# Outputs issued from ScalarE's DMA queue, and batch 1's norms from GpSimd sums, in a fused cross-covariance attention and three-way maxout FFN

## The chip, the cores and the metric

One core of one Trainium2 chip. The metric is the device time of one execution in microseconds (us). The kernel before takes 574.16 us (median of runs, 574.00 to 574.34).

## The reference, cut to what matters

```python
# q, k, v: (4, 6144, 256) float32; w1, w2, w3: (256, 768); w_out: (768, 256)
qn = q / (norm(q, axis=1) + 1e-6);  kn = k / (norm(k, axis=1) + 1e-6)
a  = softmax(kn.T @ qn / tau)                    # 256 x 256 a batch
x  = (v @ a).reshape(24576, 256)
out = max(x @ w1, x @ w2, x @ w3) @ w_out        # float32
```

The kernel folds `a` into the three weights (the "ew" products give `aw`), so a token needs only `v @ aw` and the output product. The tokens of a batch come in 12 chunks of 512. The Gram matrix `k.T @ q` of the next batch (one burst of products) and its norms are worked out while the chunks of this batch run.

## The kernel before

The steps that matter, cut (`...` marks cuts). Each engine executes its own instructions in the order in which this code issues them.

```python
def norms(b):                                # used for batch 1 only
    n_ps = htile("n_ps")
    accq, acck = accs.pop((b, 0)), accs.pop((b, 1))
    PE.matmul(n_ps[:, :C], lhsT=ones_f, rhs=acck[:, 0:C], ...)
    for j in range(CC):
        PE.matmul(n_ps[:, C + j:C + j + 1], lhsT=accq[:, j * P:(j + 1) * P], rhs=ones_f[:, 0:1], ...)
    ln = sm.tile([P, C + CC], FP32, name="ln")
    ...
def sum_all(b):                              # norms of batches 2 and 3
    ...
    POOL.partition_all_reduce(tot, acc[:, 0:C], P, bass_isa.ReduceOp.add)

def h_block(gi, aw, fc, ...):                # six of these a chunk
    for m in range(3):
        ... PE.matmul(h_ps, lhsT=aw[m][:, ic, fsl], rhs=vt[:, tsl, ic, :], ...)      # 2 x 512 columns
    ACT.activation(out=s_mx, in_=hp[0], func=AF.Copy)                 # "h copy"
    DVE.tensor_tensor(out=s_mx, in0=hp[1], in1=s_mx, op=ALU.max)      # first maximum
    DVE.tensor_tensor(out=ht, in0=hp[2], in1=s_mx, op=ALU.max)        # second maximum

def step(t):                                 # output product, t = 0..3, one in each gap between h blocks
    ...
    if t % 2 == 1:
        ACT.activation(out=st["o"][:, t - 1:t + 1, :], in_=st["ps"], func=AF.Copy)   # "o copy"
    if t == TPC - 1:
        parts = 2 if gi >= B * NCH - 7 else 1
        for i in range(parts):
            SP.dma_start(out=out_r[...], in_=st["o"][:, i * w:(i + 1) * w, :])

def v_transpose(gi):                         # SBUF to SBUF, through the DMA
    SP.dma_start_transpose(out=vt_tile(gi), in_=v_sb.rearrange("p t c -> p (t c)"))
...
if gi == 1:
    hold_loads(2)     # GpSimd copies one element of vt(2): it issues no load before transpose 2 has landed
    load_v(4); load_v(5)
...
l0 = ch if early else ch - 1                 # early = b > 0
if more and 0 <= l0 < 8:
    load_k(b + 1, l0 * 6, 6); load_q(b + 1, l0 * 6, 6)       # cast to fp8, issued by GpSimd
s0 = ch - 2 if early else ch - 3             # the first squares of batch 1 stand in chunk 3
...  square_piece(b + 1, which, g)           # ScalarE squares 3 token groups, GpSimd adds them up
```

Six PSUM buffers hold the h products (two blocks). SBUF pools are laid out one after the other in the order in which they are opened: the small tiles (`sm`, with `ln`), then `v`, `vt`, `ht`, `mx`, `o`.

## Time and profile before

| | before |
|---|---|
| time, us | 574.16 |
| profiled span, us (granted clock) | 572.1 (1.000) |
| TensorE's waits that come after the first batch's loads | none over 0.3 us |
| outputs of ScalarE's / SyncE's queue, MB (of 25.2 written) | 0.1 / the rest |

The page's third part lists DMA queues as packets, MB, and the share of 16 engines' time that the packets took. Before, transposes and outputs share SyncE's queue, and ScalarE has one output, the last:

```profile
q1 hardware_dynamic: 57696, 38.41, 23.7%
q10 hardware_dynamic: 144, 0.13, 0.1%
```

The lines of TensorE's busy share, its chain and its waits are in the prediction below.

### The profile page before, as it was taken

How to read it: one execution, taken by the hardware profiler on the slowest of the kernel's cores; microseconds unless marked ns; L12 is line 12 of the kernel's file. 1: busy time of each engine (PE TensorE's matmuls, PEld its weight loads, DVE VectorE, ACT ScalarE, POOL GpSimd, SP SyncE). 2: the span in 40 equal slices, each digit the busy share in tenths (PEclk: the TensorE clock that was granted, in tenths of full speed). 3: DMA queues.
4: the chain of work that ended last, by engine and by line, in shares of the span. 5: the costliest groups of instructions: out<-in, count | busy, mean ns of one | idle time of the engine just before them, and what ended most of it. 6: DMA issues, size and time to landing. Idle time of an engine off the chain costs nothing.

```text
span 572.1 us, 9442 instructions
## 1 busy us (share of the span) xinstructions
PE 553.9 (97%) x3349; PEld 330.7 (58%) x3350; DVE 411.1 (72%) x647; ACT 309.1 (54%) x539; POOL 235.1 (41%) x240
## 2 busy tenths in 40 slices
PE   3799999999999999999999999999999999999997
PEld 2665555555755555555575555555575555555566
DVE  0048777877577777777768777777868778778775
ACT  1044567677454576776545467767645444444443
POOL 2443357776730078776560048777750000000000
PEclk9999999999999999999999999999999999999999
DMA  9998998884598168984179339885437323132112
GB/s 143 106 146 129 136 237 126 159 135 116 99 107 160 56 107 158 134 148 110 57 128 151 99 81 140 148 141 98 124 86 154 75 75 109 56 103 64 56 55 76
DMA packets 76960, 65.64 MB, mean 115 GB/s; under 512 B 52464, under 2 KB 62576, under 8 KB 76784
## 3 DMA queue, kind: packets, MB, share of 16 engines
q0 software_dynamic: 19072, 26.48, 38.7%
q1 hardware_dynamic: 57696, 38.41, 23.7%
q8 instruction: 26, 0.43, 0.3%
q14 instruction: 22, 0.18, 0.1%
q10 hardware_dynamic: 144, 0.13, 0.1%
HBM read 78.64 MB, written 25.17 MB: 181 GB/s over the span
## 4 chain that ended last, share of the span: by engine, by line
PE 93%; DMA 5%; POOL 0%; issue 0%; DVE 0%; POOLq 0%
PE h_ps L389 65%; PE o_ps L409 22%; DMA q_sb<-in_q_dram 5%; PE gram L260 3%; PE ew_ps L311 3%; POOL k_sb L99 0%; PE o_ps L434 0%; PE ew_ps L335 0%; PE warm_ps L469 0%; PE vt_ps L372 0%; PE gram L177 0%; PE n_ps L215 0%; DVE ht_sb L395 0%; DVE o_sb L461 0%; PE n_ps L217 0%
## 5 line engine op out<-in xcount | busy, mean ns | idle before, releaser
L389 PE MATMUL h_ps<-vt_sb,aw_sb 128*128 128x512 bf16 (+1 forms) x1764 | 406.7, 375 | 0.1
L389 PEld LDWEIGHTS <-aw_sb 128*128 128x128 bf16 x1764 | 171.8, 98 | 161.3 <-DVE aw_sb L317 2.0
L394 DVE TENSOR_TENSOR s_mx<-h_ps,s_mx 128x512 bf16<-128x512 f32 (+1 forms) x294 | 198.7, 676 | 87.1 <-ACT s_mx L393 86.8
L393 ACT ACTIVATE s_mx<-h_ps 128x512 bf16<-128x512 f32 (+1 forms) x294 | 172.4, 587 | 124.9 <-PE h_ps L389 124.0
L395 DVE TENSOR_TENSOR ht_sb<-h_ps,s_mx 128x512 bf16<-128x512 f32 (+1 forms) x294 | 200.2, 681 | 31.4 <-PE o_ps L409 0.5
L203 POOL TENSOR_TENSOR acc<-acc,sq 128x768 f32<-128x768 f32 x90 | 147.6, 1651 | 70.5 <-ACT sq L197 61.6
L409 PE MATMUL o_ps<-wo_sb,ht_sb 128*128 128x256 bf16 x1128 | 153.9, 273 | 0.0
L409 PEld LDWEIGHTS <-ht_sb 128*128 128x128 bf16 x1128 | 110.4, 98 | 52.0
L412 ACT ACTIVATE o_sb<-o_ps 128x512 f32<-128x512 f32 x94 | 56.1, 597 | 85.3 <-PE o_ps L409 85.3
L110 POOL DMA_DIRECT2D v_sb<-in_v_dram x48 | 27.5, 578 | 37.7 <-DMA vt_sb<-v_sb 35.5
L197 ACT ACTIVATE sq<-q_sb 128x768 bf16<-128x768 fp8e4 x48 | 40.5, 845 | 0.0
L197 ACT ACTIVATE sq<-k_sb 128x768 bf16<-128x768 fp8e4 x48 | 40.1, 835 | 0.0
L200 POOL CAST acc<-sq 128x768 f32<-128x768 bf16 x6 | 4.9, 823 | 68.7 <-ACT sq L197 68.7
L102 POOL DMA_DIRECT2D q_sb<-in_q_dram x33 | 18.4, 564 | 5.1 <-DMA v_sb<-in_v_dram 4.1
L165 PE MATMUL kk<-k_sb 128*128 128x256 fp8e4 x48 | 7.5, 338 | 11.9 <-DVE k_sb L151 6.3
L99 POOL DMA_DIRECT2D k_sb<-in_k_dram x29 | 16.1, 555 | 3.1 <-DMA v_sb<-in_v_dram 1.2
L260 PE MATMUL gram<-k_sb,q_sb 128*128 128x512 fp8e4 x144 | 16.8, 277 | 0.0
L260 PEld LDWEIGHTS <-q_sb 128*128 128x256 fp8e4 x144 | 15.9, 136 | 0.6
L314 ACT ACTIVATE aw_sb<-ew_ps,rinv 128x384 bf16<-128x384 f32 (+1 forms) x24 | 13.2, 555 | 5.5 <-PE ew_ps L311 4.7
L311 PE MATMUL ew_ps<-w_sb,et 128*128 128x384 bf16 (+1 forms) x96 | 15.6, 313 | 0.0
L177 PE MATMUL gram<-k_sb,q_sb 128*128 128x512 fp8e4 x48 | 11.4, 332 | 2.6 <-DMA q_sb<-in_q_dram 2.4
L165 PEld LDWEIGHTS <-k_sb 128*128 128x256 fp8e4 x48 | 6.4, 182 | 12.9 <-DMA k_sb<-in_k_dram 6.6
(67 smaller groups left out, 112.9 us busy)
## 6 DMA issues: line engine op xcount, KB each, us to landing
out_dram<-o_sb SPq DMA_DIRECT2D x41, 512.0 KB, 2.9
v_sb<-in_v_dram POOLq DMA_DIRECT2D x48, 256.0 KB, 4.2
k_sb<-in_k_dram POOLq DMA_DIRECT2D x24, 192.0 KB, 6.0
q_sb<-in_q_dram POOLq DMA_DIRECT2D x24, 192.0 KB, 7.6
out_dram<-o_sb SPq DMA_DIRECT2D x13, 256.0 KB, 2.0
k_sb<-in_k_dram POOLq DMA_DIRECT2D x5, 256.0 KB, 10.8
w_sb<-in_moe_w_dram POOLq DMA_DIRECT2D x9, 128.0 KB, 5.7
kf<-in_k_dram SPq DMA_DIRECT2D x1, 1024.0 KB, 4.8
```

The costliest lines, as they stand in the source:

```text
L102: POOL.dma_start(out=qk[b][0][:, g0:g0 + w, :], in_=q_r[b][:, g0:g0 + w, :])
L110: POOL.dma_start(out=t, in_=v_r[gi // NCH, gi % NCH])
L197: ACT.activation(out=sq, in_=src, func=AF.Square)
L203: POOL.tensor_tensor(out=acc, in0=acc, in1=sq, op=ALU.add)
L260: PE.matmul(g[:, j * C:(j + 1) * C], lhsT=qt[:, tsl, j * P:(j + 1) * P], rhs=kt[:, tsl, :], start=(tp == 0 and j == 0), stop=(tp == NG // ...
L311: PE.matmul(ew[:, :w], lhsT=et[:, j, ic * P:(ic + 1) * P], rhs=w_sb[m][:, j, fsl], start=(j == 0), stop=(j == CC - 1))
L389: PE.matmul(t.rearrange("p (t n) -> p t n", n=P), lhsT=aw[m][:, ic, fsl], rhs=vt[:, tsl, ic, :], start=(ic == 0), stop=(ic == CC - 1))
L393: ACT.activation(out=s_mx, in_=hp[0], func=AF.Copy)
L394: DVE.tensor_tensor(out=s_mx, in0=hp[1], in1=s_mx, op=ALU.max)
L395: DVE.tensor_tensor(out=ht, in0=hp[2], in1=s_mx, op=ALU.max)
L409: PE.matmul(st["ps"][:, half], lhsT=ht[:, fc, t * P:(t + 1) * P], rhs=wo_sb[:, fc, :], start=(fc == 0), stop=(fc == FC - 1))
L412: ACT.activation(out=st["o"][:, t - 1:t + 1, :].rearrange("p t d -> p (t d)"), in_=st["ps"], func=AF.Copy)
```

## The change

The intent: SyncE's queue is free of outputs, so that an output no longer stands behind a blocked transpose issue; and the fp32 norm products of batch 1 leave TensorE, which bounds the kernel. For the second, batch 1's squares begin a chunk earlier (chunk 2), so that GpSimd's sums are ready by the Gram burst.

```diff
-    def norms(b):
-        n_ps = htile("n_ps")
-        ...                                  # the n_ps products, the tile ln, three activations
-    def norms_all(b):
+    def norms(b):                            # now for all batches, from sum_all
...
-                    SP.dma_start(out=out_r[gi // NCH, gi % NCH, :, i * w:(i + 1) * w, :],
+                    ACT.dma_start(out=out_r[gi // NCH, gi % NCH, :, i * w:(i + 1) * w, :],
...
+            pieces = [(which, g) for g in range(0, NG, SQW) for which in (1, 0)]
...
-            s0 = ch - 2 if early else ch - 3
-            ...
+            if more and 2 <= ch < 10:
+                at = {2: (3, 4, 5), 3: (0, 1, 2, 3, 5)}.get(ch, (0, 2, 3, 5)) if b == 0 else (0, 2, 3, 5)
+                for f in at:
+                    which, g = pieces.pop(0)
+                    gaps[f].append(lambda which=which, g=g: square_piece(b + 1, which, g))
+                if ch == 9:
+                    gaps[5].append(lambda: (fold(b + 1), sum_all(b + 1)))
```

More of the change, by code (lines that the diff above doesn't have):

```diff
@@ L209, in fold @@
                 POOL.tensor_tensor(out=acc[:, 0:C], in0=acc[:, 0:C], in1=acc[:, i * C:(i + 1) * C], op=ALU.add)
-    def norms(b):
-        n_ps = htile("n_ps")
-        accq, acck = accs.pop((b, 0)), accs.pop((b, 1))
-        PE.matmul(n_ps[:, :C], lhsT=ones_f, rhs=acck[:, 0:C], start=True, stop=False, skip_group_check=True)
-        for j in range(CC):
-            PE.matmul(n_ps[:, C + j:C + j + 1], lhsT=accq[:, j * P:(j + 1) * P], rhs=ones_f[:, 0:1],
-                      start=False, stop=(j == CC - 1), skip_group_check=True)
-        ln = sm.tile([P, C + CC], FP32, name="ln")
-        rkb = sm.tile([P, C], FP32, name="rkb")
-        rq = sm.tile([P, CC], FP32, name="rq")
-        ACT.activation(out=ln, in_=n_ps[:, :C + CC], func=AF.Ln)
-        ACT.activation(out=rkb, in_=ln[:, :C], func=AF.Exp, scale=-0.5)
-        ACT.activation(out=rq, in_=ln[:, C:], func=AF.Exp, scale=-0.5, bias=neg_ln_tau)
-        return rkb, rq
     def sum_all(b):
@@ L504 @@
             v_transpose(gi + 3)
-            early = b > 0
-            l0 = ch if early else ch - 1
+            l0 = ch if b > 0 else ch - 1
             if more and 0 <= l0 < 8:
@@ L518 @@
                 gaps[s + 1].append(f)
-            s0 = ch - 2 if early else ch - 3
-            if more and 0 <= s0 < 8:
-                g0 = s0 * 6
-                for i, (which, g) in enumerate(((1, g0), (1, g0 + SQW), (0, g0), (0, g0 + SQW))):
-                    gaps[(0, 2, 3, 5)[i]].append(lambda which=which, g=g: square_piece(b + 1, which, g))
-            if more and s0 == 7:
-                gaps[5].append(lambda: fold(b + 1))
-                if early:
-                    gaps[5].append(lambda: sum_all(b + 1))
-            if more and ch == NCH - 1:
-                if early:
-                    st["in"] = scaled(gs, st["n"][0])
-                    gaps[0].append(lambda: st.update(e=exp_t(st["in"], st["n"][1])))
-                else:
-                    gaps[0].append(lambda: st.update(n=norms(b + 1)))
-                    gaps[1].append(lambda: st.update({"in": scaled(gs, st["n"][0])}))
-                    gaps[2].append(lambda: st.update(e=exp_t(st["in"], st["n"][1])))
+            if more and 2 <= ch < 10:
[5 more added lines that the diff above has]
+                    gaps[5].append(lambda: (fold(b + 1), sum_all(b + 1)))
+            if more and ch == NCH - 1:
+                st["in"] = scaled(gs, st["n"][0])
+                gaps[0].append(lambda: st.update(e=exp_t(st["in"], st["n"][1])))
                 gaps[4].append(lambda: st.update(r=rowsums(st["e"])))
@@ L543 @@
                 st = {}
-                if early:
-                    st["n"] = norms_all(b + 1)
+                st["n"] = norms(b + 1)
                 gs = gram_kq(b + 1)
```

## The prediction

> **What bounds the kernel now.** I read the page first, then TensorE's waits, then the order of time in four places: a quiet chunk, a batch boundary, the start and the end.
>
> ```profile
> PE 553.9 (97%) x3349; PEld 330.7 (58%) x3350; DVE 411.1 (72%) x647; ACT 309.1 (54%) x539; POOL 235.1 (41%) x240
> PE 93%; DMA 5%; POOL 0%; issue 0%; DVE 0%; POOLq 0%
> PE kk L165 <- DVE k_sb L151: 6.3, 1, 6.3
> PE kk L165 <- DMA k_sb<-in_k_dram: 5.7, 5, 1.6
> PE gram L177 <- DMA q_sb<-in_q_dram: 2.4, 3, 1.2
> ```
>
> TensorE is busy 97% of 572.1 us, the chain that ended last lies on it for 93%, and its whole list of waits is these three lines, all at the first batch's loads. The strip of the granted clock reads 9 in every slice, so throttling is out. A matmul of 512 columns starts every 0.216 us (six take 1.29 us in the chain). From about 37 to 560 us the kernel lasts as long as TensorE's own instructions. Only two things can change the time: fewer TensorE instructions, or new holes between them. ScalarE at 54% looks free, but the share does not say how late one of its copies may be.
>
> **What the Trainium skill says.** "Perfetto Trace Analysis", section "DMA Instruction — HWDGE (DVE, Sync)": the profiler reports a DMA issue until the sequencer is free for its next instruction, and before that the sequencer takes the descriptor generator for itself alone. The first half fits: SyncE's issues take 0.33 us here and its next instruction comes about 0.1 us later. The lock is not shown: at the end an issue of SyncE starts inside one of ScalarE and still takes 0.33 us. "DMA: Bandwidth & Descriptors", section "Issuing engines are not separate DMA queues": issuing from another engine saves only the issue time. So nothing moves faster for coming from ScalarE. The same page, section "Queues, rings and completion order": each DMA engine takes turns between queues, packet by packet. The start agrees: one transpose issue takes 13.83 us while GpSimd's casting loads fill the engines.
>
> **Part 1, batch 1's norms: a gain of 0.8 us.** The n_ps products go (three in the code; the trace records each of these fp32 products twice):
>
> ```profile
> 157.19 1.47 PE L389 MATMUL h_ps<-vt_sb,aw_sb 128*128 128x512 bf16 x6
> 158.49 0.59 PE L215 MATMUL n_ps<-acc,ones_f 128*128 128x256 f32 x2
> 158.92 0.50 PE L217 MATMUL n_ps<-ones_f,acc 128*128 128x1 f32 x4
> 159.29 1.45 PE L389 MATMUL h_ps<-vt_sb,aw_sb 128*128 128x512 bf16 x6
> ```
>
> From 158.49 to 159.29 is 0.80 us. It can be checked: from the start of the Gram burst to the first regular block of three takes 152.10 to 181.70 = 29.60 us for batch 1, but 286.90 to 315.70 = 28.80 us for batch 2, which already uses the GpSimd sums. In batch 2 ScalarE waits 4.9 us for the sums, inside a burst of 5.24 us, and TensorE does not notice. The new work on GpSimd (two all-reduces of 1.81 and 1.88 us) is hidden likewise.
>
> **Part 2, outputs on ScalarE: a loss.** 46 chunks now store from ScalarE's in-order stream, between the second copy of the output and the next h copy:
>
> ```profile
> 480.72 4.05 PE L389 MATMUL h_ps<-vt_sb,aw_sb 128*128 128x512 bf16 x18
> 480.92 0.60 ACT L412 ACTIVATE o_sb<-o_ps 128x512 f32<-128x512 f32 x1 [0.92 <-PE o_ps L409]
> 481.41 0.59 ACT L393 ACTIVATE s_mx<-h_ps 128x512 bf16<-128x512 f32 x1
> 481.54 0.33 SPq L418 DMA_DIRECT2D out_dram<-o_sb  x1
> 482.03 0.69 DVE L394 TENSOR_TENSOR s_mx<-h_ps,s_mx 128x512 bf16<-128x512 f32 x1 [0.52 <-ACT s_mx L393]
> 482.83 0.69 DVE L395 TENSOR_TENSOR ht_sb<-h_ps,s_mx 128x512 bf16<-128x512 f32 x1
> ...
> 568.89 0.41 ACTq L462 DMA_DIRECT2D out_dram<-o_sb  x1
> ```
>
> The store needs the copy's end (481.52), so it starts at 481.54. ScalarE's one issue took 0.41 us, so it ends at 481.95; with 0.1 us to the next start (SyncE's gap, an estimate) the h copy starts at 482.05 in place of 481.41: 0.64 us late. Is there room? The six h buffers hold two blocks. The 18 matmuls are three blocks, and the third takes the first one's buffers. Its last pair starts at 480.72 + 16 x 0.216 = 484.17 and needs the end of the second maximum. That moves: copy 482.05 to 482.64, first maximum 482.66 to 483.35, second 483.46 to 484.15, and a hand-over of 0.02 to 0.05 us after it. The room is just used up: a hole of 0.03 us a chunk. An issue 0.1 us longer or shorter makes it 0.13 or none. With squares in the stream the offsets are the same (140.95, 142.37 against a block starting at 140.26).
>
> Counting the 46: three are followed by a Gram burst, which hides the delay; three fall at a boundary; three at the start; 37 are regular. 37 x 0.03 = 1.1 us (0 to 5).
>
> Boundaries: the sixth ew product starts at about 170.10 and waits for the second maximum of the block before it:
>
> ```profile
> 167.28 0.60 ACT L412 ACTIVATE o_sb<-o_ps 128x512 f32<-128x512 f32 x1 [0.92 <-PE o_ps L409]
> 167.81 0.60 ACT L393 ACTIVATE s_mx<-h_ps 128x512 bf16<-128x512 f32 x1
> 168.44 0.69 DVE L394 TENSOR_TENSOR s_mx<-h_ps,s_mx 128x512 bf16<-128x512 f32 x1 [0.20 <-ACT s_mx L393]
> 169.24 0.69 DVE L395 TENSOR_TENSOR ht_sb<-h_ps,s_mx 128x512 bf16<-128x512 f32 x1
> ```
>
> Now it ends at 169.93. The h copy moves from 167.81 to 168.42, the maximum's end to 170.52: 0.45 us late, three times: 1.3 us. At the end of the kernel VectorE is the bound of the last half chunk, and the same 0.6 us goes straight into the time.
>
> Start: in chunk 2 a square of 0.84 us now also stands behind the store, so the h copy is 0.64 + 0.74 (a square less its overlap) = 1.4 us late, a hole of 0.8 us; chunks 1 and 3 add some 0.3 us, as issues take 0.58 us there.
>
> Sum: -0.8 + 1.1 + 1.3 + 0.6 + 1.1 = +3.3 us, or 577.6 us.
>
> **Rivals.** First, all fits and only the gain remains: 573.5 us. For it: every delay but the boundaries' is within 0.1 us of its room, and only one issue on ScalarE has been measured. Against it: the boundaries and the end have no room at all.
>
> Second, the descriptor generator is taken for the whole of a blocked transpose issue, as the skill words it:
>
> ```profile
> 58.27 0.60 POOL L99 DMA_DIRECT2D k_sb<-in_k_dram  x1
> 61.39 0.61 SPq L418 DMA_DIRECT2D out_dram<-o_sb  x1
> 62.13 13.83 SPq L365 DMA_TRANSPOSE vt_sb<-v_sb  x1
> 76.01 0.58 SPq L418 DMA_DIRECT2D out_dram<-o_sb  x1
> ```
>
> Chunk 1's store falls due near 68.35, inside that issue. ScalarE would stand until the transpose gets through, by my estimate near 73 us (batch 1's third pair of loads now comes behind GpSimd's first sums, so the load queue runs dry earlier than in the kernel before). The hole would be about 5 us in place of 0.8: 582 us. For it: 13.83 us shows that such a block exists. Against it: ScalarE has its own queue, and the overlap of issues at the end.
>
> Third, the squares, one chunk earlier, wait for their loads. Batch 1's first k load was issued at 56.71 and landed 8.2 us later, near 64.9; the first square now comes due at 64.91, with 0.46 us of room before the next h copy. Later a load has a whole chunk of 10.4 us against 6.0 to 7.6 us to landing. I expect under 0.5 us from it, 576 to 580 us in all if it goes wrong.
>
> **Range and chances.** I give the first rival 3 in 10, my sum 4 in 10, the blocked start 3 in 10: a middle of 577.0 us and a range of 573.2 to 583.0 us. Only 0.8 us of TensorE's work goes, so faster by over 2% (562.8) has no source: 0.01. Slower by over 2% (585.8) needs regular holes of 0.25 us or a blocked start longer than estimated: 0.06. Within 2%: 0.93.
>
> **What would show it.** Right: n_ps is gone and the first boundary is 0.8 us shorter but for a hole of some 0.45 us before the sixth ew product; about 47 output issues of 0.4 us on ScalarE; new lines in TensorE's waits naming VectorE's second maximum, a few hundredths of a us in regular chunks, the largest one near 70 us. The second rival: one ScalarE issue of several us near 68. The third: ScalarE's squares waiting for k or q loads. Wrong: issues on ScalarE well away from 0.41 us, TensorE's waits unchanged, or a changed granted clock.

## The result, and the profile after

The changed kernel takes 578.36 us (578.13 to 578.61, four runs) against 574.16: ratio 1.0073 (95% interval 1.0056 to 1.0091), so the same within 2%, and 0.7% slower. A ratio here is the mean time of one kernel's fast runs over that of the other's in the same rounds, so not quite the ratio of the medians quoted. Executions over 1.5% slower than the fastest of the same kernel are left out of the means. The profiled span grew from 572.1 to 576.8 us, 4.7 us.

The page of the changed kernel (busy us, share, instructions; the chain that ended last; the queues):

```profile
PE 555.2 (96%) x3344; PEld 328.9 (57%) x3344; DVE 409.3 (71%) x651; ACT 311.5 (54%) x540; POOL 238.4 (41%) x242
PE 85%; DMA 8%; issue 3%; DVE 1%; POOL 1%; ACT 0%; POOLq 0%; DVEq 0%
q1 hardware_dynamic: 50064, 13.77, 14.4%
q10 hardware_dynamic: 7776, 24.78, 11.7%
```

24.65 MB of outputs (24.78 - 0.13) have moved from SyncE's queue to ScalarE's. TensorE has the same work to do. Its share of the chain fell by 8 points, 46 us, far more than the 4.7 us lost: from the late load at 69 us (below) the chain now runs back through DMA, the transposes and GpSimd, and no longer through TensorE. TensorE's list of waits, beside those for the first loads, now has three lines that the kernel before lacks (us in total, times, longest):

```profile
PE h_ps L373 <- ACT s_mx L377: 1.4, 4, 0.8
PE h_ps L373 <- DVE aw_sb L301: 0.7, 3, 0.2
PE h_ps L373 <- DVE ht_sb L379: 0.2, 1, 0.2
```

They are the places where the time went, but not all of it: a list of waits counts from the modelled end of the product before. I therefore went through TensorE's products in order and added up by how much each start-to-start distance exceeds the usual one of its kind (0.216 us for 512 columns), in both traces. The difference of the two sums, place by place:

| place | us |
|---|---|
| n_ps products gone | -0.80 |
| first loads (before 40 us; the first h product starts at 37.5 to 38.1 us in the six traces, so it differs from run to run) | +0.54 |
| the wait for wo_sb, the weights of the output product, at 51.4 us | +0.19 |
| the start, 70 to 74 us | +2.30 |
| the three batch boundaries (0.57, 0.58, 0.58 against 0.055 each) | +1.56 |
| the end (1.46 against 0.55) | +0.91 |
| regular chunks: no hole over 0.02 us | 0 |
| sum | +4.70 |

The sum is the whole difference of the spans; without the first loads it is 4.16, and the medians differ by 4.20. The three places, one by one.

**The start.** ScalarE's and TensorE's order of time around 70 us (start, us, engine, line, what, and in brackets how long it stood idle and for what); the last line is the kernel before at the same place:

```profile
69.11 0.84 ACT L197 ACTIVATE sq<-k_sb 128x768 bf16<-128x768 fp8e4 x1 [3.47 <-DMA k_sb<-in_k_dram]
70.96 0.34 ACTq L402 DMA_DIRECT2D out_dram<-o_sb  x1
71.41 0.84 ACT L197 ACTIVATE sq<-q_sb 128x768 bf16<-128x768 fp8e4 x1 [0.49 <-DMA q_sb<-in_q_dram]
```

```profile
68.26 1.46 PE L373 MATMUL h_ps<-vt_sb,aw_sb 128*128 128x512 bf16 x6
70.49 1.32 PE L373 MATMUL h_ps<-vt_sb,aw_sb 128*128 128x512 bf16 x4 [0.77 <-ACT s_mx L377]
```

```profile
67.53 4.05 PE L389 MATMUL h_ps<-vt_sb,aw_sb 128*128 128x512 bf16 x18
```

ScalarE stood 3.47 us before batch 1's first square, because its k load had not landed; h copy, o copy and the output stood behind it, and TensorE, whose 18 products ran in one piece before, was held by the missing h copy. This load was issued at 59.06 us and landed at 69.09; before, it was issued at 56.71 and landed at 64.89. It is both issued 2.35 us later and 1.85 us longer under way. The experiments take up why.

During all this SyncE was inside one transpose issue:

```profile
63.93 11.03 SPq L349 DMA_TRANSPOSE vt_sb<-v_sb  x1
```

ScalarE's issue at 70.96 lies in the middle of it and took 0.34 us. So here the issue of one engine did not wait for the blocked issue of another.

**The boundaries.** ScalarE, VectorE and TensorE at the first boundary after the change; the last fence is TensorE before:

```profile
170.15 0.34 ACTq L402 DMA_DIRECT2D out_dram<-o_sb  x1
170.59 0.60 ACT L377 ACTIVATE s_mx<-h_ps 128x512 bf16<-128x512 f32 x1 [0.47 <-PE h_ps L373]
172.62 1.66 DVE L301 TENSOR_SCALAR aw_sb<-ew_ps,rinv 128x384 bf16<-128x384 f32 x3
173.29 1.44 PE L373 MATMUL h_ps<-vt_sb,aw_sb 128*128 128x512 bf16 x5 [0.24 <-DVE aw_sb L301]
```

```profile
170.43 1.52 PE L389 MATMUL h_ps<-vt_sb,aw_sb 128*128 128x512 bf16 x6
```

No ew product waits: the sixth pair starts at 172.34 us, before the second maximum of the block before it has ended (172.70). The issue makes the h copy late, the h copy makes VectorE's two maxima late, and VectorE's scaling of the new weights comes after them in its order. The next batch's first products need those weights: the run of six is broken after its first product.

**The end.** The last two runs of products, TensorE and ScalarE after, TensorE before:

```profile
560.09 0.38 PE L373 MATMUL h_ps<-vt_sb,aw_sb 128*128 128x256 bf16 x2 [0.23 <-ACT s_mx L377]
565.10 0.96 ACTq L402 DMA_DIRECT2D out_dram<-o_sb  x2
566.16 0.66 ACT L377 ACTIVATE s_mx<-h_ps 128x256 bf16<-128x256 f32 x2 [0.47 <-PE h_ps L373]
566.59 3.42 PE L373 MATMUL h_ps<-vt_sb,aw_sb 128*128 128x256 bf16 x24 [0.23 <-ACT s_mx L377]
```

```profile
553.45 2.77 PE L389 MATMUL h_ps<-vt_sb,aw_sb 128*128 128x512 bf16 x18
560.64 4.63 PE L389 MATMUL h_ps<-vt_sb,aw_sb 128*128 128x256 bf16 x36
```

There are two places. At 560.09, where the products turn from 512 to 256 columns and a run of 18 was in one piece before, there is now a hole of 0.42 us. In the last half chunk the 36 products in one piece have become 12 and 24 with a hole between, and smaller holes follow inside the 24 (1.04 us in all, against 0.55 before). Two output issues stand ahead of the h copy of 566.16, but they cost no more than one: the first (565.10 to 565.44) falls within the o copy of 565.09 to 565.69, and the h copy starts 1.07 us after the o copy, as in a regular chunk (1.06, below).

**A regular chunk.** Near 485 us:

```profile
484.76 0.60 ACT L396 ACTIVATE o_sb<-o_ps 128x512 f32<-128x512 f32 x1 [0.92 <-PE o_ps L393]
485.38 0.34 ACTq L402 DMA_DIRECT2D out_dram<-o_sb  x1
485.82 1.26 ACT L377 ACTIVATE s_mx<-h_ps 128x512 bf16<-128x512 f32 x2 [0.47 <-PE h_ps L373]
```

The h copy starts 1.06 us after the o copy in place of 0.49: 0.57 us late. TensorE does not notice.

### The profile page after: what moved, and what is told of

It is laid out like the page before. It is cut to its first block, busy times and chain, and to the rows that moved or that the text cites. A ratio compares the mean times of both kernels' runs of the same rounds, so it can differ in the third digit from the quotient of the medians.

```text
span 576.8 us, 9433 instructions
## 1 busy us (share of the span) xinstructions
PE 555.2 (96%) x3344; PEld 328.9 (57%) x3344; DVE 409.3 (71%) x651; ACT 311.5 (54%) x540; POOL 238.4 (41%) x242
## 3 DMA queue, kind: packets, MB, share of 16 engines
q10 hardware_dynamic: 7776, 24.78, 11.7%
## 4 chain that ended last, share of the span: by engine, by line
PE 85%; DMA 8%; issue 3%; DVE 1%; POOL 1%; ACT 0%; POOLq 0%; DVEq 0%
PE h_ps L373 61%; PE o_ps L393 20%; DMA v_sb<-in_v_dram 4%; PE gram L244 3%; DMA k_sb<-in_k_dram 2%; DMA vt_sb<-v_sb 1%; PE ew_ps L295 1%; DMA q_sb<-in_q_dram 1%; DVE s_mx L378 1%; DVE ht_sb L379 0%; POOL k_sb L99 0%; PE o_ps L418 0%; ACT s_mx L377 0%; DVE aw_sb L301 0%; POOL v_sb L110 0%
## 5 line engine op out<-in xcount | busy, mean ns | idle before, releaser
L110 POOL DMA_DIRECT2D v_sb<-in_v_dram x48 | 27.7, 583 | 28.1 <-DMA vt_sb<-v_sb 25.9
L216 POOL PARTITION_ALL_REDUCE tot<-acc x6 | 10.8, 1844 | 18.2 <-issue 12.1
```

The costliest lines, as they stand in the source:

```text
L110: POOL.dma_start(out=t, in_=v_r[gi // NCH, gi % NCH])
```

## The experiments

The first four ran on one chip, beside 11 runs of the kernel before (median 574.06 us, 573.84 to 574.49).

**store_sp: the change without the move of the outputs.**

```diff
-                    ACT.dma_start(out=out_r[...],
+                    SP.dma_start(out=out_r[...],
```

> The changed kernel with its output stores back on SyncE; the norms from GpSimd and the early squares stay. My theory (a store in ScalarE's stream makes the next h copy about 0.57 us late, and chunk 1's output in a queue of its own holds up batch 1's first k load): the holes of 0.52 us at the three boundaries and of 0.9 us at the end are gone, the k load lands some 8 us after its issue instead of 10, and the hole of 2.3 us near 70 us shrinks to under 0.3 us: 573.4 us, 0.8 us below the kernel before. Rival 1, the boundary holes come from the removed n_ps product, which changed the order of the PSUM buffers: they stay, 575 us. Rival 2, the squares come too early whatever the queue: most of the 2.3 us stays, 575.5 us.

Measured: 573.43, 573.53, 573.59 and 573.65 us in four runs, 581.48 in the profiled one and 597.35 in one that counts as slow; ratio of the fast runs 1.0018 (0.9977 to 1.0059), so the same within 2% as the kernel before. In its trace the boundaries have no hole over 0.1 us, the end has 0.55 us again, and there is no hole near 70 us: the boundary and end losses belong to the outputs' place in ScalarE's stream. The load landed 7.65 us after its issue, and the first square waited 1.00 us for it, though the squares stood as early as in the changed kernel. The four good runs have no trace. Their mean, 573.55 us, is 4.8 us below the changed kernel's time, and the start, the boundaries and the end together lost 4.77, so by their times all three losses are gone. They lie 0.5 us below the kernel before; 0.8 was expected from n_ps. The profiled run lost its time elsewhere, in a way that no run of the kernel before or of the changed one shows in its time:

```profile
98.42 0.84 ACT L197 ACTIVATE sq<-k_sb 128x768 bf16<-128x768 fp8e4 x1 [6.05 <-DMA k_sb<-in_k_dram]
99.80 1.01 PE L373 MATMUL h_ps<-vt_sb,aw_sb 128*128 128x512 bf16 x2 [4.39 <-ACT s_mx L377]
101.89 2.67 PE L373 MATMUL h_ps<-vt_sb,aw_sb 128*128 128x512 bf16 x6
```

A square waited 6.05 us for its load, TensorE stood 4.39 us behind it, and after that six products took 2.67 us in place of 1.46: the granted clock was 0.5 for some 6.8 us. That agrees with the Trainium skill, "TensorE: Matmul & The Clock Gate", section "What's actually happening", by which the clock falls to half after an idle window of about 3.4 us; shorter holes (1.48 us at 84.9 us in the same trace) left it at 1. The DMA queues of 85 to 100 us go one step further back, first this run, then the kernel before (packets, MB, share of 16 engines):

```profile
q1 hardware_dynamic: 2302, 1.55, 85.5%
```

```profile
q1 hardware_dynamic: 1200, 0.79, 19.7%
```

The packets of transposes and outputs took 0.855 x 15 us x 16 / 2302 = 89 ns each, against 39 ns. Sorted by size in the trace, it is the transposes' 256-byte packets that are longer: 82.9 ns in the mean against 24.0 (and 27.7 in the changed kernel); the outputs' packets of 4096 bytes took 166 ns against 174. The loads beside them landed 14 to 18 us after their issue in place of 4 to 8. I call this the congested state below.

**store_only: only the move, in the kernel before.**

```diff
-                    SP.dma_start(out=out_r[...],
+                    ACT.dma_start(out=out_r[...],
```

> The kernel before with nothing but its output stores moved to ScalarE. My theory: boundary holes of about 0.5 us three times and about 0.9 us at the end, no hole near 70 us because no square waits for an early load there: 574.2 + 1.5 + 0.9 = 576.6 us. If the stores alone made the start hole as well (an issue that blocks, or chunk 2's late copy), 578.9 us. If the boundary holes come from the removed product, 575.1 us.

Measured: 578.44, 580.96, 581.08, 581.44 us, and 588.51 in the profiled run (slow); ratio 1.0111 (1.0095 to 1.0127). The trace has the holes of the boundaries (0.51, 0.57, 0.57) and of the end (1.72, against 1.46 in the changed kernel), so they need nothing of the norms. But the time misses the expected 576.6: the best run is 1.8 us above it. The profiled run was congested as well. One square waited 8.44 us for a k load, and TensorE behind it:

```profile
155.26 1.01 PE L389 MATMUL h_ps<-vt_sb,aw_sb 128*128 128x512 bf16 x2 [7.34 <-ACT s_mx L393]
```

The trace also shows what can have lifted the best run. At 81.3 us there is a hole of 2.05 us, in which TensorE waited for a transposed v tile, as it never does in the kernel before:

```profile
PE h_ps L389 <- DMA vt_sb<-v_sb: 1.9, 1, 1.9
```

That transpose landed at 81.25 us (78.33 before). An estimate from these traces, 574.06 + 1.48 (boundaries) + 0.91 to 1.17 (end) + 2.05, gives 578.5 to 578.8 us, and the best run took 578.44; it has no trace, so this is a fit and no more.

**late_squares: the changed kernel with batch 1's first squares back in chunk 3.**

```diff
-                at = {2: (3, 4, 5), 3: (0, 1, 2, 3, 5)}.get(ch, (0, 2, 3, 5)) if b == 0 else (0, 2, 3, 5)
+                at = {2: (), 3: (0, 1, 2, 3, 5), 4: (0, 1, 2, 3, 5), 5: (0, 1, 2, 3, 5), 6: (0, 1, 2, 3, 5)}.get(ch, (0, 2, 3, 5)) if b == 0 else (0, 2, 3, 5)
```

> The changed kernel, but batch 1's squares start in chunk 3 as in the kernel before (five in each of chunks 3 to 6, four in 7 to 9), stores stay on ScalarE. My theory: the hole of 2.3 us near 70 us goes and the rest stays: 578.3 - 2.3 = 576.0 us. Rival, the store of chunk 1 or 2 blocks ScalarE by itself: the hole stays, 578 us. A second way to miss: five squares a chunk crowd ScalarE or GpSimd and the sums arrive after the Gram burst, over 578 us.

Measured: 577.74, 578.11, 581.03, 585.94 us, and two slow runs of 586.51 and 591.07, the latter profiled; ratio 1.0115 (1.0072 to 1.0158). A miss as a time. In the trace the hole near 70 us is gone, as expected; in its place stand others. Those from 109 us on, one of 7.15 us at 127 us, come behind squares that wait for their loads (8.5 us at the most), that is, the congested state. The first, 2.33 us at 82.2 us, is that of store_only again, a transpose that landed at 82.17:

```profile
PE h_ps L373 <- DMA vt_sb<-v_sb: 2.2, 1, 2.2
```

So in this trace the loss of the start was not gone but had moved, from a square's load to a transpose, at the same size. The best two runs, 577.74 and 578.11, gain only 0.3 to 0.6 us on the changed kernel, which fits that; they have no trace.

**late_squares_sp: the same with the outputs back on SyncE.**

```diff
-                    ACT.dma_start(out=out_r[...],
+                    SP.dma_start(out=out_r[...],                # and the edit of late_squares
```

> Both undone: stores on SyncE and the squares from chunk 3, only the norms from GpSimd stay. All theories: the 0.80 us of the removed product alone, 573.4 us or a ratio of 0.9986 to the kernel before; first boundary 28.8 us from the start of the Gram burst to the first regular block of three. If it isn't below the kernel before, the gain of the removed product was given back elsewhere in the burst.

Measured: 584.90, 585.19, 586.77, 589.05 us and a slow 597.31; ratio 1.0215 (1.0194 to 1.0237), a verdict of unclear at the bound of 2%. The clearest miss: no run came near the 573.5 us of store_sp, whose outputs it has. It differs from store_sp only in where the squares stand, and by its times it lost over 10 us in all five runs, where store_sp did so in one of six and 8 us in another. So the squares' places bear on the congested state; how is not shown. In the trace ScalarE waits 15.1 us in four places for k loads, and TensorE has holes between 80 and 127 us, but none at the boundaries.

**What these four leave.** They settle the boundaries and the end. For the start, the three traces with outputs from ScalarE lose 2.30, 2.05 and 2.33 us before 85 us, by a late square or a late transpose; with outputs from SyncE none is lost near 70 us in any, and at the transposes' place near 80 us none in two traces and 0.65 in late_squares_sp (store_sp's congestion begins at 84.9). They don't say why the changed kernel's first load comes late. Two things can be read side by side from the six traces.

First, the transposes. SyncE's first transpose runs alone, and the second holds up GpSimd, which issues batch 1's first load only after its guard copy. In the kernel before, the first takes (us from issue to landing), and the guard copies stand at (first and last start):

```profile
vt_sb<-v_sb SPq DMA_TRANSPOSE x1, 2.9
L480 POOL COPY guard<-vt_sb x2: 185/186/188, 45.1 to 54.7; 128x1 bf16<-128x1 bf16 x2
```

In the changed kernel, the first, the second, and the guard copies:

```profile
vt_sb<-v_sb SPq DMA_TRANSPOSE x1, 3.2
vt_sb<-v_sb SPq DMA_TRANSPOSE x1, 4.3
L464 POOL COPY guard<-vt_sb x2: 183/186/188, 46.0 to 57.0; 128x1 bf16<-128x1 bf16 x2
```

| kernel | start of the v tiles, bytes (past a 256-byte line) | first transpose: ns a packet, us to landing | second: us to landing |
|---|---|---|---|
| before | 144640 (0) | 17.9, 2.88 | 2.76 |
| store_only | 144640 (0) | 17.9, 2.87 | 2.82 |
| changed | 142528 (192) | 21.6, 3.21 | 4.29 |
| store_sp | 142528 (192) | 21.6, 3.18 | 4.22 |
| late_squares | 142528 (192) | 21.7, 3.23 | 4.32 |
| late_squares_sp | 142528 (192) | 21.5, 3.20 | 4.20 |

The kernels fall into two groups, and what divides them is not the place of the outputs or of the squares but whether `ln` is there. That tile took 2 x 1056 bytes ahead of the v and vt tiles; without it each 256-byte row of a transpose begins 192 bytes past a 256-byte line. The Trainium skill, "DMA: Bandwidth & Descriptors", section "How a descriptor splits into AXI transactions", says that a transaction must start from a 256-byte-aligned address, so a descriptor that begins between two of them starts with a transaction at the line below, of which part is thrown away: by that rule a row of 256 bytes needs two transactions. The 1024 packets of the first transpose, all of 256 bytes and alone on the engines, agree in direction: 21.6 against 17.9 ns, a fifth more and not double. The guard copy comes 2.3 us later than before (57.0 against 54.7): 0.8 us because this run issued the second transpose later (52.63 against 51.81; about 0.5 of it stood at 42 us already, 0.33 is the first transpose's), and 1.5 us because the transpose took longer. Longer packets alone gave the first transpose 0.33 us. The rest of the 1.5 goes along with something else: in the four traces without `ln` the third transpose's packets run among the second's (1754 to 1790 packets of 29 to 32 ns before the second lands), in the other two hardly (about 1200 of 17.8 ns). What brings that on is not shown. The wo_sb load, behind the first guard copy, is late as well: TensorE waited 0.13 to 0.29 us for it at 51 us in these four, and not in the other two. The first load comes later by the same 2.3 us (59.06 against 56.71).

That the alignment is the cause is argued from six traces, not shown by an experiment on it. The one meant to show it could not be had:

**after_padded (not run).** The changed kernel with the v tiles put on a 256-byte line again.

```diff
+    pad = ctx.enter_context(tc.tile_pool(name="pad", bufs=1))
+    pad.tile([P, 16], FP32, name="pad")
     v_pool = ctx.enter_context(tc.tile_pool(name="v", bufs=6))
```

> The changed kernel with 64 unused bytes a partition ahead of the v tiles. The change dropped the tile ln (2 x 1056 bytes), which moved v and vt from a 256-byte boundary (144640, 156928) to 192 bytes past one (142528, 154816); the 64 bytes put them on a boundary again (142592, 154880). If the alignment makes the transposes slow: packets of 18 ns in place of 22, the second transpose lands about 2.8 us after its issue in place of 4.2, batch 1's first k load is issued about 57 us and lands about 66 in place of 69, the first square waits under 1 us in place of 3.5, the hole near 70 us shrinks from 2.3 to 0.8 us or less: 576.7 us (576.3 to 577.2). Boundary holes (1.56) and end (1.46) stay. If something else slows the transposes: landing still 4.2 us after issue, and 578.4 us.

The size of the alignment's part in the 2.30 us, and whether a later issue of the outputs closes the holes of the boundaries and the end, stay untested. What store_sp does show is that the misaligned tiles and the early squares, without outputs on ScalarE, lost nothing near 70 us.

Second, the outputs in a queue of their own. Where ScalarE issues the outputs, batch 1's first k load takes 10.0 (changed), 9.2 (store_only) and 9.3 us (late_squares) to land; where SyncE does, 8.2 (before), 7.7 (store_sp) and 8.1 us (late_squares_sp). Chunk 0's output (the expectation of store_sp calls it chunk 1's) landed only at 79.42 us before, on SyncE's queue with the transposes; in the changed kernel, in a queue of its own, it was under way from 58.69 to 66.36 us. This is the taking of turns that the prediction quotes: the trace of the changed kernel has 119 packets of 4096 bytes of ScalarE's queue among GpSimd's 146 packets of 2048 bytes at 62 to 65 us. (The 13.83 us that the prediction gives as agreeing show a long issue, not taking turns.) This too is read from traces that differ in nothing else of the start but the outputs, for two pairs (before and store_only, changed and store_sp); a third pair, late_squares and late_squares_sp, agrees. Each kernel has one trace.

## Why the prediction was right

The time was right: 577.0 us with a range of 573.2 to 583.0, and 578.36 came out, in the class that had 0.93. By its own steps:

- **The gain of 0.8 us** held: the n_ps products are gone, and GpSimd's new sums stay hidden (ScalarE waits for a sum three times, 5.0 us at the most, within the bursts; TensorE never).
- **Regular chunks, 37 x 0.03 us:** the mechanism held to the last step, the size did not. The issue took 0.34 us, not the 0.41 of the one record on hand, so the h copy is 0.57 us late in place of 0.64, and a room of about 0.60 is enough. The term was 1.1 us and is 0. "The room is just used up" was a sum of ten durations against a margin of hundredths: it could only say that the term was near the edge.
- **Boundaries, 3 x 0.45 us:** the delay is real and the size nearly right (0.52 each), the place was not. The step "the sixth ew product starts at about 170.10 and waits for the second maximum" failed: no ew product waits. The delay runs on through VectorE's order to the scaling of the new weights, and the next batch's first products wait for those. An engine's order had to be followed one instruction further.
- **The end, 0.6 us:** 0.91, in two places of which the step had one. In the last half chunk, which the step had, 0.49 came of the h copy's 0.58 us; the other 0.42 stand at 560.09, where the blocks of 256 columns begin. The step "about 47 output issues" overlooked that these chunks store in two halves (53 issues of the moved outputs); that cost nothing, as the first half's issue falls within the o copy.
- **The start, 1.1 us:** 2.30, by another mechanism. The step took the output and a square, both in time, as what makes the h copy late, with issues of 0.58 us; they took 0.37 and 0.34. What happened is the third rival, which was allowed "under 0.5 us": the first square waits 3.47 us for its load. That estimate took the load's landing from the kernel before (64.9 us), as if the change could not move it; it landed at 69.09.
- **The second rival**, a generator locked for the length of a blocked transpose issue, is refuted by the issue of 0.34 us at 70.96.

So the sum of +3.3 us came near the +4.2 of the medians partly by luck (574.16 + 3.3 is 577.5, not 577.6, which changes nothing): a term that was too large (regular chunks, +1.1 against 0) made up for one that was too small (start, 1.1 against 2.3).

**What stays open.** The congested state of 80 to 165 us is in the profiled runs of all four variants, and by their times in other runs of theirs, but by their times in none of the 4 runs of the changed kernel or the 15 of the kernel before. It comes with outputs on either queue and with v tiles on either alignment, so neither is its cause alone. Which timing of loads, transposes and outputs brings it on was not found. And the late first load at the start has two causes that the traces suggest, the misaligned transposes and the outputs' own queue. The second was tested by single edits, in one trace each; the first was not tested. The pairs of traces give about 1.5 us (1.8 with the first transpose's delay) to the first and 1.0 to 2.4 us to the second, out of 4.2 us by which the load lands later, of which about 0.5 was there from the first loads on.

## What to carry to other kernels

A store at the end of an engine's in-order stream costs that engine its issue (0.34 us here) plus the wait for its source; look for what stands behind it, and follow the delay through the next engine's order until something with no room is reached. It was free here in the middle of a steady loop with some 0.6 us of room (an estimate, from the prediction's sum), and showed up at the seams: the first iterations, the batch boundaries and the end. An output that leaves a queue of waiting transposes also moves earlier than it did, among the loads and transposes of the start. And when a tile is removed, look at where the tiles after it now lie.

## What the Trainium skill lacked or had wrong

- "Perfetto Trace Analysis", section "DMA Instruction — HWDGE (DVE, Sync)" says that the descriptor generator is locked for exclusive use by an issue. Between two engines no such lock shows here, or it isn't held for the whole of an issue: ScalarE's issue at 70.96 us took 0.34 us inside SyncE's transpose issue of 63.93 to 74.96 us.
- "DMA: Bandwidth & Descriptors" gives the 256-byte rule for a descriptor's transactions, but its section "DMA Transpose (X-bar)" asks only for 32-byte alignment. Tiles 192 bytes past a 256-byte line come with 21.6 ns a packet in place of 17.9, and 3.2 us in place of 2.9 for one transpose by itself.
- The same page's "Issuing engines are not separate DMA queues" says that another issuing engine saves only the sequencer's time. In three pairs of traces it also went with a change of when other transfers landed: batch 1's first load took 9.2 to 10.0 us beside outputs on ScalarE's queue and 7.7 to 8.2 us beside outputs on SyncE's.
- No page tells of a state in which transposes and the loads beside them are slow for tens of us in some runs only: 82.9 ns for a 256-byte packet of a transpose in place of 24.0, loads landing after 14 to 18 us in place of 4 to 8.
